# Turning query features one feed-forward unit later, with two query tiles instead of four in the last phase

## The chip, the cores and the metric

The kernel runs on one core of a Trainium2 chip. The time is device microseconds of the whole execution on that core, the median of several runs; a profile is one further execution, with its own time.

## What is computed

A linear attention with learned softmax features and a gated feed-forward layer, both on the same normalised input, for 2048 tokens of width 640, 32 heads of width 20, and a hidden width of 1536:

```python
xn = _layernorm(x, axis=-1)
# attention: q, k, v from xn @ wqkv; per head
pq = einsum("bhsd,hdf->bhsf", q, w_phi);  pk = einsum("bhsd,hdf->bhsf", k, w_phi)
phi_q = concat([softmax(pq), softmax(-pq)]);  phi_k = concat([softmax(pk), softmax(-pk)])
kv = einsum("bhsf,bhsd->bhfd", phi_k, v);  z = einsum("bhsf->bhf", phi_k)
o = einsum("bhqf,bhfd->bhqd", phi_q, kv) / (einsum("bhqf,bhf->bhq", phi_q, z)[..., None] + 1e-6)
s = o @ wo
# feed-forward
g = silu(gelu(xn @ w1 + b1) @ w2 + b2)
return x + s * g
```

## The kernel before

The program has three phases. Products of fp32 values are made from a high and a low part each (three matmuls, `PASSES`), so most operands are slabs with two halves.

**First phase**: normalisation, keys, values and queries of 16 tiles of 128 tokens. A query tile ends as exponentials in DRAM (`e_dram`). The sums over the keys (`kvp`) build up in one PSUM bank.

**Feed-forward phase**: 12 units, `unit` = 6 * h + g. Half h is one half of the tokens, group g two of the twelve blocks of the hidden width. A unit computes the hidden values in seven parts (`part`, L649, one Strassen-like scheme over two token groups and two blocks) and then the down projection (`down`, L678) for two token groups into `ys`. Between the matmuls, the loop's body calls generators, each up to its next `yield`, so that the other engines' work stands at fixed places in program order:

- `q_norm(t, ef)` turns the exponentials of query tile t into normalised features: `ez` on GpSimd (L724), sums on VectorE (L365), the reciprocal of the denominator, scaling on GpSimd (L370), a transpose on VectorE (L741), and four stores to `phi_t` on SyncE's queue (L745). `q_load` (L718) fetches the exponentials. `QN` says which tiles are turned in which unit.
- `w1_forms` makes the next unit's five W1 tiles on ScalarE (L429) and GpSimd (L418, L430). Units 2 to 4 also store theirs (`w1_store`, L445), and units 7 to 9 fetch them back for the unit that follows (`w1_back`, L451).
- `x_forms` makes, in units 0 to 3, sums of the input for the second half, stored by L711 and L712; `reload` fetches the second half's input in unit 5.

**Last phase**: four blocks of 512 tokens in the order `ORDER = (2, 3, 0, 1)`. `load_phi` (L764, L766) loads a block's features; `num` (L776, L783) multiplies them with the state of the keys into `oT` (VectorE's half is L780); `finish` (L829 to L836) makes one of five output tiles of a block: 16 matmuls with `wo`, the product with the gate (L831), the sum with the input (L832), the store (L836). For the blocks 2 and 3 the gates come from DRAM (`gt`), for 0 and 1 from `ys`. `load_res` asks for input and gate two tiles ahead. Between the tiles `late_q` turns the last query tiles, a step for every `next(lq)`. `load_wol` loads the last rows of `wo` and makes their low part.

From the feed-forward phase on, all engines run in the order in which the program is written (`manual_schedule`), with semaphores for the data. All loads and stores of this part are issued by SyncE, in program order: an instruction that waits for its data holds all behind it. Slabs (`slab`, 23 of them), rows (11) and PSUM banks (8) are pools: a new tile waits until an earlier one's last reader is done.

Of the kernel before, what the change touches and what calls it, by code (L numbers as in the profile page):

```python
# [15 lines left out]
P = 128  # L16
NT = S // P
NCH = 4
# [28 lines left out]
def hedgehog_gated_mlp_kernel(ctx: ExitStack, tc: tile.TileContext, x, xt_in, wqk, bd, wv, wo, w1, b1, w2, b2, out_t):  # L47
# [33 lines left out]
    def slab(dt, name, shape=(P, 2, D)):  # L81
        return slabs.tile(list(shape), dt, tag="S", name=name)

    def row(shape, dt, name):
        return rows.tile(shape, dt, tag="R", name=name)
# [4 lines left out]
    def bankB(name="pB"):  # L90
        return pools["B"].tile([P, 512], F32, tag="B", name=name)
# [271 lines left out]
    def head_sums(ef, tag):  # L363
        ss = small.tile([P, 64], F32, tag=tag, name=tag)
        nc.vector.tensor_reduce(ss[:], ef.rearrange("p (g d) -> p g d", d=DH), axis=AX.X, op=OP.add)  # L365
        return ss

    def scale_heads(ef, rc):
        e3 = ef.rearrange("p (g d) -> p g d", d=DH)
        nc.gpsimd.tensor_tensor(e3, e3, rc[:, :, None].to_broadcast([P, 64, DH]), op=OP.mult)  # L370
# [67 lines left out]
    def w1_dict(tiles):  # L438
        wa, wc, wd, wb = tiles
        return dict(A11=(wa, 0), A12=(wa, 256), A1k=(wa, 512), A22=(wb, 0), A2k=(wb, 256),  # L440
                    S1=(wc, 0), S2=(wc, 256), S3=(wd, 0), S4=(wd, 256), tiles=tiles)
# [5 lines left out]
    def w1_back(g):  # L447
        out = []
        for o, n in W1OFF:
            sl = slab(F32R, "w1s")  # L450
            nc.sync.dma_start(sl[:, :, :n].bitcast(F32), w1_dram[g][:, :, o:o + n])  # L451
            out.append(sl)
        return w1_dict(out)
# [139 lines left out]
    t = NT - 1  # L593
# [121 lines left out]
    def q_load(t):  # L715
        e = slab(F32, "eq")
        ef = e[:].rearrange("p a b -> p (a b)")
        nc.sync.dma_start(ef, e_dram[t])  # L718
        return ef

    def q_norm(t, ef):
        ez = slab(F32, "ez")
        zv = ez[:].rearrange("p a b -> p (a b)")
        nc.gpsimd.tensor_tensor(zv, ef, zf, op=OP.mult)  # L724
        yield
        rc = head_sums(ef, "rc")
        nc.vector.reciprocal(rc[:], rc[:])
        yield
        dn = head_sums(zv, "dn")
        yield  # L730
        nc.vector.tensor_tensor(dn[:], dn[:], rc[:], op=OP.mult)
        d3 = dn[:].rearrange("p (h s) -> p h s", s=2)
        den = small.tile([P, 32], F32, tag="den", name="den")
        nc.vector.scalar_tensor_tensor(den[:], d3[:, :, 0], DEN_EPS, d3[:, :, 1], op0=OP.add, op1=OP.add)
        nc.vector.reciprocal(den[:], den[:])
        r3 = rc[:].rearrange("p (h s) -> p h s", s=2)
        nc.vector.tensor_tensor(r3, r3, den[:, :, None].to_broadcast([P, 32, 2]), op=OP.mult)  # L737
        yield
        scale_heads(ef, rc)
        yield  # L740
        nc.vector.transpose(ef, ef)  # L741
        c, i = divmod(t, TPC)
        dst = phi_t[c].rearrange("(b j) (t a i) -> t a j b i", j=32, a=4, i=32)[i]
        for a in range(4):
            nc.sync.dma_start(dst[a], ef[32 * a:32 * a + 32, :].rearrange("p (b i) -> p b i", i=32))  # L745

    def load_wol():
        raw = row([P, D], F32, "raw")
        for r in range(3):
            nc.sync.dma_start(raw[40 * r:40 * r + 40, :], wo[640:680, :])  # L750
        wol_h = row([P, D], F32R, "wolh")
        wol = row([P, D], F32R, "wol")
        nc.vector.tensor_copy(wol_h[:120, :], raw[:120, :])
        nc.vector.scalar_tensor_tensor(wol[:120, :], wol_h[:120, :].bitcast(F32), midsel[:120, :], raw[:120, :],
                                       op0=OP.mult, op1=OP.add)
        return wol


    def load_phi(c, js):
        out = {}  # L760
        for j in js:
            ph = slab(F32, "phT", (P, 2, CW))
            if j < 5:
                nc.sync.dma_start(ph[:120], phi_t[c][240 * j:240 * j + 240, :].rearrange("(e p) t -> p e t", p=120))  # L764
            else:
                nc.sync.dma_start(ph[:80, 0], phi_t[c][1200:, :])  # L766
            out[j] = ph
        return out
# [20 lines left out]
    JA, JB = (0, 1, 2), (3, 4, 5)  # L789
# [2 lines left out]
        return ([home.tile([P, 2, 512], F32R, tag="S" if home is slabs else "L", name="oT") for _ in range(5)],  # L792
                slab(F32R, "oTl", (P, 2, 512)))

    xres, gates = {}, {}
    ORDER = (2, 3, 0, 1)

    def load_res(i):
# [18 lines left out]

    def finish(c, d, oT, last):
        steps = [(wo_s[j][:, b, d * P:(d + 1) * P], oT[0][j][:, a, :]) for j in range(5) for a, b in PASSES]
        steps.append((wol[:120, d * P:(d + 1) * P], oT[1][:120, 1, :]))  # L820
        xr, gt = xres.pop((c, d)), gates.pop((c, d))
        end = last and d == KC - 1
        parts = (slice(0, 384), slice(384, 512)) if end else (slice(0, W2), slice(W2, 512))
        for k, sl in enumerate(parts):
            if end or k == 0:
                mv = sl if end else slice(0, 512)
                ps = bankB()
                for n, (w, o) in enumerate(steps):
                    nc.tensor.matmul(ps[:, mv], w, o[:, mv], start=n == 0, stop=n == 15, skip_group_check=True)  # L829
            g = gt[:, sl]  # L830
            nc.vector.tensor_tensor(g, ps[:, sl], g, op=OP.mult)  # L831
            (nc.vector if last else nc.gpsimd).tensor_tensor(xr[:, sl], g, xr[:, sl], op=OP.add)  # L832
            if last:
                nc.sync.dma_start(out_t[d * P:(d + 1) * P, c * CW + sl.start:c * CW + sl.stop], xr[:, sl])
        if not last:
            nc.sync.dma_start(out_t[d * P:(d + 1) * P, c * CW:(c + 1) * CW], xr[:])  # L836


    zf, none = None, iter(())
    QN = {1: (8,), 2: (9,), 3: (10,), 4: (11,), 5: (12,), 7: (13, 14), 8: (15, 0), 9: (1, 2), 10: (3,)}  # L840
    units = NH * NG

    def w2_raw(g):
        return [load_raw(w2[f * P:(f + 1) * P, :]) for f in range(g * GF, (g + 1) * GF)]
# [6 lines left out]
    open_psum(ctx, B=8)  # L851
    ffn = ExitStack()
    ffn.enter_context(tc.manual_schedule())
    qe, xg, qlast = {}, none, none
    for unit in range(units):
        h, g = divmod(unit, NG)
        f1, f2 = g * GF, g * GF + 1
        more, back = unit + 1 < units, NG + 1 < unit + 1 < units - 1
        qs = [q_norm(t, qe.pop(t)) for t in QN.get(unit, ())]
        q1, q2 = (qs + [none, none])[:2]  # L860
        next(q1, None)
# [9 lines left out]
            wo_r = [load_raw(wo[j * P:(j + 1) * P, :]) for j in range(5)]  # L871
            phi = load_phi(ORDER[0], range(6))
        xo, xg = xg, (x_forms(unit, *x_back(unit)) if unit < SLOTS else none)
        for t in QN.get(unit + 1, ()):
            qe[t] = q_load(t)
        if 2 <= unit < NG - 1:
            w1_store(unit, w1g)
        if unit == NG + 1:
# [39 lines left out]
        h21 = act_lo(*h21)  # L918
        nc.vector.tensor_tensor(c12, u2[:], c12, op=OP.add)
        h12 = act(c12, f1)  # L920
        next(qlast, None)
        qlast = q2
        next(xo, None)
        silu(3)
        hs = ((h11, h21), (None, h22))
# [9 lines left out]
        w1f = w1_forms(w1r) if more and not back else none  # L935
        if back:
            w1g = w1_back((unit + 1) % NG)
        next(w1f, None)
        dn = down(g, w2g, hs, 0)
        next(dn)  # L940
# [23 lines left out]
        next(dn)  # L964
        next(dn)
        next(q2, None)
        next(q1, None)
        next(dn)
        next(q2, None)
        next(dn)  # L970
# [1 line left out]
        if unit == NG - 1:  # L972
            held = list(ys)
            ys[:] = [None] * KC
    wol = load_wol()
    oT = new_oT(late)
    phin = load_phi(ORDER[1], JA)
    qe[4] = q_load(4)
    load_res(0)
    load_res(1)  # L980

    def first_num():
        num(phi, oT, JA)
        yield
        yield
        num(phi, oT, JB)
        yield
# [5 lines left out]
    gate(1)  # L993

    def late_q():
        qn = q_norm(4, qe.pop(4))
        next(qn)
        for t in range(4, 8):
            if t < 7:
                qe[t + 1] = q_load(t + 1)  # L1000
            next(qn)
            yield
            next(qn)
            yield
            next(qn)
            next(qn)
            yield
            next(qn, None)
            if t < 7:
                qn = q_norm(t + 1, qe.pop(t + 1))  # L1010
                next(qn)
            yield

    lq = late_q()
    for ci, c in enumerate(ORDER):
        if ci + 1 < NCH:
            oTn = new_oT(late if ci % 2 else slabs)
        for d in range(KC):
            load_res(ci * KC + d + 2)
            finish(c, d, oT, ci == NCH - 1 and d >= 3)  # L1020
            next(lq, None)
            gate(ci * KC + d + 2)
            if ci == 0 and d % 2 == 0:
                next(lq, None)
            if ci + 1 < NCH and d in (1, 3):
                num(phin, oTn, JA if d == 1 else JB)
            if ci + 2 < NCH and d >= 3:
                phin.update(load_phi(ORDER[ci + 2], JA if d == 3 else JB))
            next(lq, None)
        if ci + 1 < NCH:  # L1030
            oT = oTn
    ffn.close()
# [50 lines left out]
```

## Time and profile before

| | |
|---|---|
| median of 3 runs | 694.87 us (690.53 to 695.24) |
| profiled execution, its own time | 692.98 us |
| its span, first to last instruction | 691.2 us |
| TensorE busy | 666.4 us (96%) |
| mean granted TensorE clock | 0.984 |
| DMA moved | 126.05 MB |

In the views, PE is TensorE (PEld its weight loads), DVE VectorE, ACT ScalarE, POOL GpSimd, SPq SyncE's queue of DMA issues. A line of a timeline has start, duration, engine, source line, operation, tiles, count, and in brackets the idle time before it and what ended it. A line of the chain of waits has start, duration and the piece of work. A line of waits says who waited for whom, for how long in total, how often, and the longest.

### The profile page before, as it was taken

How to read it: one execution, taken by the hardware profiler on the slowest of the kernel's cores; microseconds unless marked ns; L12 is line 12 of the kernel's file. 1: busy time of each engine (PE TensorE's matmuls, PEld its weight loads, DVE VectorE, ACT ScalarE, POOL GpSimd, SP SyncE). 2: the span in 40 equal slices, each digit the busy share in tenths (PEclk: the TensorE clock that was granted, in tenths of full speed). 3: DMA queues.
4: the chain of work that ended last, by engine and by line, in shares of the span. 5: the costliest groups of instructions: out<-in, count | busy, mean ns of one | idle time of the engine just before them, and what ended most of it. 6: DMA issues, size and time to landing. Idle time of an engine off the chain costs nothing.

```text
span 691.2 us, 11372 instructions
## 1 busy us (share of the span) xinstructions
PE 666.4 (96%) x4447; PEld 572.1 (83%) x4447; DVE 468.9 (68%) x720; ACT 227.2 (33%) x321; POOL 380.8 (55%) x351
## 2 busy tenths in 40 slices
PE   8999999999999999999898999999999999969798
PEld 8999999999999988887676888888888866636476
DVE  5787576878776567598566884578988646784222
ACT  3513213333233254424333247533134251103120
POOL 3653355767756486583858762726546542753231
PEclk9999999999999999999999999999999999989899
DMA  8820325451631536049587799465876699699943
GB/s 327 305 77 2 60 91 160 162 149 78 156 124 63 172 118 227 25 107 354 128 292 215 204 421 330 160 224 157 200 187 161 135 247 275 183 259 244 267 142 108
DMA packets 157950, 126.05 MB, mean 182 GB/s; under 512 B 88656, under 2 KB 125520, under 8 KB 157000
## 3 DMA queue, kind: packets, MB, share of 16 engines
q1 hardware_dynamic: 155592, 114.84, 57.8%
q10 hardware_dynamic: 2304, 10.49, 4.1%
q8 instruction: 35, 0.57, 0.3%
q14 instruction: 19, 0.16, 0.1%
HBM read 80.20 MB, written 45.10 MB: 181 GB/s over the span
## 4 chain that ended last, share of the span: by engine, by line
PE 69%; DMA 14%; DVE 6%; SPq 5%; POOL 3%; issue 2%; ACT 0%; DVEq 0%; POOLq 0%; ACTq 0%
PE pA L331 27%; PE pB L649 17%; PE pB L678 17%; DMA phT<-phi_t 6%; PE pB L829 5%; DMA w_dram<-w1s 2%; SPq L745 2%; DMA xt<-in_x_dram 2%; PE kv L402 2%; POOL w1s L430 1%; DVE eq L741 1%; POOL eq L370 1%; DMA folds<-in_wqk_dram 1%; DMA raw<-in_wv_dram 1%; DVE y L687 1%
## 5 line engine op out<-in xcount | busy, mean ns | idle before, releaser
L678 PE MATMUL pB<-hs,w2s 128*128 128x512 f32 x720 | 166.1, 390 | 1.2 <-DVE oT L780 1.2
L678 PEld LDWEIGHTS pB<-hs,w2s 128*128 128x128 f32 x720 | 135.3, 188 | 31.0 <-DVE oT L780 2.1
L649 PE MATMUL pB<-xp,w1s 128*128 128x512 f32 x324 | 85.2, 402 | 6.6 <-DVE pB L910 5.2
L649 PEld LDWEIGHTS pB<-xp,w1s 128*128 128x128 f32 x324 | 62.4, 194 | 21.3 <-DVE pB L910 6.0
L649 PE MATMUL pB<-xd,w1s 128*128 128x512 f32 x324 | 79.3, 389 | 0.0
L829 PE MATMUL pB<-oT,wo 128*128 128x512 f32 (+2 forms) x315 | 76.1, 394 | 2.7 <-DVE oT L780 2.7
L829 PEld LDWEIGHTS pB<-oT,wo 128*128 128x128 f32 x315 | 59.3, 194 | 20.5 <-DVE oT L780 4.0
L649 PEld LDWEIGHTS pB<-xd,w1s 128*128 128x128 f32 x324 | 60.8, 188 | 12.7
L357 ACT ACTIVATE e<-e 128x1280 f32<-128x1280 f32 x32 | 40.7, 1272 | 91.2 <-POOL e L352 90.7
L687 DVE TENSOR_TENSOR y<-pB,y 128x512 f32<-128x512 f32 x100 | 63.4, 677 | 5.4 <-PE pB L678 5.4
L370 POOL TENSOR_TENSOR eq<-eq,rc 128x1280 f32<-128x1280 f32 x16 | 37.9, 2371 | 50.0 <-DVE rc L737 40.7
L370 POOL TENSOR_TENSOR e<-e,rc 128x1280 f32<-128x1280 f32 x16 | 39.0, 2438 | 47.6 <-DVE rc L390 47.4
L352 POOL TENSOR_TENSOR e<-nr,e 128x640 f32<-128x640 f32 x32 | 44.2, 1383 | 30.8 <-DVE nr L351 25.9
L331 PE MATMUL pA<-wv,xp 128*128 128x320 f32 x384 | 60.5, 310 | 0.3 <-POOL wv L147 0.3
L331 PE MATMUL pA<-wk,xp 128*128 128x320 f32 x384 | 59.7, 310 | 0.0
L654 ACT ACTIVATE pB<-pB,b1t 128x512 f32<-128x512 f32 x48 | 31.8, 662 | 83.4 <-DVE pB L910 33.6
L331 PE MATMUL pA<-wq,xp 128*128 128x320 f32 x384 | 58.8, 309 | 0.2 <-DVE nr L351 0.2
L331 PEld LDWEIGHTS pA<-wv,xp 128*128 128x128 f32 x384 | 57.0, 188 | 0.5 <-POOL wv L147 0.5
L331 PEld LDWEIGHTS pA<-wq,xp 128*128 128x128 f32 x384 | 56.9, 188 | 0.4 <-PE pA L331 0.4
L331 PEld LDWEIGHTS pA<-wk,xp 128*128 128x128 f32 x384 | 56.9, 188 | 0.1
L724 POOL TENSOR_TENSOR ez<-eq,zrep 128x1280 f32<-128x1280 f32 x16 | 47.2, 2950 | 1.2 <-issue 1.2
L430 POOL TENSOR_TENSOR w1s<-raw,w1s 128x640 fp32r<-128x640 f32 (+1 forms) x18 | 25.7, 1429 | 28.0 <-ACT w1s L429 23.8
(138 smaller groups left out, 997.1 us busy)
## 6 DMA issues: line engine op xcount, KB each, us to landing
raw<-in_w_dram SPq DMA_DIRECT2D x42, 320.0 KB, 4.1
e_dram<-e ACTq DMA_DIRECT2D x16, 640.0 KB, 3.4
eq<-e_dram SPq DMA_DIRECT2D x16, 640.0 KB, 6.2
phi_t<-eq SPq DMA_DIRECT2D x64, 160.0 KB, 3.7
phT<-phi_t SPq DMA_DIRECT2D x20, 480.0 KB, 11.4
xt<-in_x_dram SPq DMA_DIRECT2D x16, 320.0 KB, 5.2
xres<-in_xt_dram SPq DMA_DIRECT2D x20, 256.0 KB, 6.0
out_dram<-xres SPq DMA_DIRECT2D x18, 256.0 KB, 5.8
```

Of the source, the lines that this page charges most:

```text
L331: nc.tensor.matmul(ps[:, hf, :HALF], stat_x(q, o, k, a), ws[k][:, b, hf * HALF:(hf + 1) * HALF], start=n == 0, stop=n == 3 * KC - 1)
L352: nc.gpsimd.tensor_tensor(e5[:, :, :, 1, :], nr[:, :, :, None].to_broadcast([P, 2, 16, DH]), e5[:, :, :, 0, :], op=OP.subtract)
L357: nc.scalar.activation(ef, ef, AF.Exp)
L370: nc.gpsimd.tensor_tensor(e3, e3, rc[:, :, None].to_broadcast([P, 64, DH]), op=OP.mult)
L402: nc.tensor.matmul(ps[32 * e:32 * e + 32, 40 * s:40 * s + 40], v[:, 21 * h:21 * h + 32], phi[:, 40 * h:40 * h + 40], start=t == 0 and s == ...
L430: nc.gpsimd.tensor_tensor(sl[:, 1, :n], src, sl[:, 0, :n].bitcast(F32), op=OP.subtract)
L649: nc.tensor.matmul(bank[ch][:], tl[:, a, off + wo_:off + wo_ + P], mov(blk, b), start=new and n == 0, stop=n == len(mms) - 1, skip_group_c ...
L654: nc.scalar.activation(ps, ps, AF.Gelu_apprx_tanh, bias=b1t[:, f:f + 1])
L678: nc.tensor.matmul(ps[:], ws[i][:, b, d * P:(d + 1) * P], hs[o][i][:, a, :], start=i == n == 0, stop=(i, n) == (GF - 1, 2), skip_group_che ...
L687: nc.vector.tensor_tensor(y, ps[:], y, op=OP.add)
L724: nc.gpsimd.tensor_tensor(zv, ef, zf, op=OP.mult)
L829: nc.tensor.matmul(ps[:, mv], w, o[:, mv], start=n == 0, stop=n == 15, skip_group_check=True)
```

## The change

The last steps of `q_norm` are split: the transpose and the four stores are now separate steps, and both are taken in the unit after the one that did the rest (`turn(qdone)` twice, in the middle of the unit: the transposes after the last activation, the stores after the W1 forms of the next unit have been asked for). The loads of the next unit's queries move from the start of a unit to the place behind these stores. Tiles 4 and 5, which were turned in the last phase, are turned in units 10 and 11, so that `late_q` finishes tile 5 and turns 6 and 7. The steps of `late_q` are called at other places, the features of the third and fourth block are loaded at a block's tiles 1 and 3, and the raw rows of `wol` are loaded in unit 11 and made into `wol` between the first two groups of query products.

```diff
@@ q_norm
         nc.vector.transpose(ef, ef)
+        yield
         c, i = divmod(t, TPC)
...
-    def load_wol():
+    def wol_raw():
         raw = row([P, D], F32, "raw")
         for r in range(3):
             nc.sync.dma_start(raw[40 * r:40 * r + 40, :], wo[640:680, :])
+        return raw
+
+    def make_wol(raw):
...
-    QN = {1: (8,), 2: (9,), 3: (10,), 4: (11,), 5: (12,), 7: (13, 14), 8: (15, 0), 9: (1, 2), 10: (3,)}
+    QN = {1: (8,), 2: (9,), 3: (10,), 4: (11,), 5: (12,), 7: (13, 14), 8: (15, 0), 9: (1, 2), 10: (3, 4), 11: (5,)}
+
+    def turn(qs):
+        for q in qs:
+            next(q, None)
@@ the loop over the units
         xo, xg = xg, (x_forms(unit, *x_back(unit)) if unit < SLOTS else none)
-        for t in QN.get(unit + 1, ()):
-            qe[t] = q_load(t)
         if 2 <= unit < NG - 1:
             w1_store(unit, w1g)
...
         h12 = act(c12, f1)
-        next(qlast, None)
-        qlast = q2
+        turn(qdone)
         next(xo, None)
...
         if back:
             w1g = w1_back((unit + 1) % NG)
+        if not more:
+            wolr = wol_raw()
+        turn(qdone)
+        qdone = qs
+        for t in QN.get(unit + 1, ()):
+            qe[t] = q_load(t)
         next(w1f, None)
         dn = down(g, w2g, hs, 0)
...
         next(q2, None)
-        next(q1, None)
         next(dn)
@@ after the loop
-    wol = load_wol()
     oT = new_oT(late)
     phin = load_phi(ORDER[1], JA)
-    qe[4] = q_load(4)
+    qe[6] = q_load(6)
...
     def first_num():
         num(phi, oT, JA)
         yield
+        wols.append(make_wol(wolr))
         yield
...
     def late_q():
-        qn = q_norm(4, qe.pop(4))
+        turn(qdone)
+        turn(qdone)
+        qn = q_norm(6, qe.pop(6))
         next(qn)
-        for t in range(4, 8):
-            if t < 7:
-                qe[t + 1] = q_load(t + 1)
+        qe[7] = q_load(7)
+        yield
+        for t in (6, 7):
...
+            next(qn)
+            yield
             next(qn, None)
...
@@ the loop over the blocks
             next(lq, None)
             gate(ci * KC + d + 2)
-            if ci == 0 and d % 2 == 0:
+            if ci == 0 and d < 4 or ci == 1 and d == 0:
                 next(lq, None)
             if ci + 1 < NCH and d in (1, 3):
                 num(phin, oTn, JA if d == 1 else JB)
-            if ci + 2 < NCH and d >= 3:
-                phin.update(load_phi(ORDER[ci + 2], JA if d == 3 else JB))
-            next(lq, None)
+            if ci + 2 < NCH and d in (1, 3):
+                phin.update(load_phi(ORDER[ci + 2], JA if d == 1 else JB))
```

More of the change, by code (lines that the diff above doesn't have):

```diff
@@ L793, in new_oT @@
                 slab(F32R, "oTl", (P, 2, 512)))
-    xres, gates = {}, {}
+    xres, gates, wols = {}, {}, []
     ORDER = (2, 3, 0, 1)
@@ L819, in finish @@
         steps = [(wo_s[j][:, b, d * P:(d + 1) * P], oT[0][j][:, a, :]) for j in range(5) for a, b in PASSES]
-        steps.append((wol[:120, d * P:(d + 1) * P], oT[1][:120, 1, :]))
+        steps.append((wols[0][:120, d * P:(d + 1) * P], oT[1][:120, 1, :]))
         xr, gt = xres.pop((c, d)), gates.pop((c, d))
@@ L853, in hedgehog_gated_mlp_kernel @@
     ffn.enter_context(tc.manual_schedule())
-    qe, xg, qlast = {}, none, none
+    qe, xg, qdone = {}, none, []
     for unit in range(units):
@@ L1007, in late_q @@
             yield
+            next(qn)
+            yield
             next(qn, None)
-            if t < 7:
-                qn = q_norm(t + 1, qe.pop(t + 1))
+            if t == 6:
+                qn = q_norm(7, qe.pop(7))
                 next(qn)
```

## The prediction

> **What bounds the kernel now.** I read the page's first parts, then the busy time cut at the starts of the feed-forward units (each unit begins with the first L649 matmul of its seven parts), then TensorE's timeline for its gaps, then the chain of waits behind each gap, then SyncE's queue and the DMA share.
>
> ```profile
> span 691.2 us, 11372 instructions
> PE 666.4 (96%) x4447; PEld 572.1 (83%) x4447; DVE 468.9 (68%) x720; ACT 227.2 (33%) x321; POOL 380.8 (55%) x351
> ...
> 326.80:358.62 31.82, 28.04 (x116) 22.38 (x115) 21.46 (x32) 10.96 (x18) 21.57 (x19) 0.95 0.78 232
> 358.62:389.47 30.85, 28.03 (x116) 22.41 (x114) 20.49 (x30) 11.76 (x19) 27.38 (x23) 0.94 0.67 200
> 519.04:544.88 25.84, 25.84 (x116) 21.40 (x115) 23.00 (x34) 8.98 (x15) 20.45 (x15) 1.00 0.52 121
> 544.88:570.70 25.82, 25.82 (x115) 18.16 (x113) 10.97 (x18) 11.57 (x19) 8.93 (x6) 1.00 1.00 237
> ```
>
> The columns of a stretch are its length, then busy time of PE, PEld, DVE, ACT, POOL, the granted clock, the DMA share and GB/s. TensorE is the bound: a unit that never waits (519.04, unit 10) is 25.84 us of matmuls end to end. Only what keeps TensorE idle or at a lower clock can be won. Units 3 and 4 take 31.82 and 30.85 us: 3.78 and 2.82 us idle, and the same 116 matmuls took 28.04 instead of 25.84.
>
> ```profile
> 341.24 3.88 PE L649 MATMUL pB<-xp,w1s 128*128 128x512 f32 x9 [2.60 <-DVE pB L910]
> 372.11 3.91 PE L649 MATMUL pB<-xp,w1s 128*128 128x512 f32 x9 [2.57 <-DVE pB L910]
> ...
> 572.30 5.74 PE L678 MATMUL pB<-hs,w2s 128*128 128x512 f32 x24 [1.19 <-DVE oT L780]
> 585.25 2.79 PE L776 MATMUL pB<-phT,bdk 120*64 120x512 f32 x12
> 607.39 1.69 PE L829 MATMUL pB<-oT,wo 128*128 128x512 f32 x4 [2.74 <-DVE oT L780]
> 617.79 4.67 PE L776 MATMUL pB<-phT,bdk 120*64 120x512 f32 x12 [3.71 <-DMA phT<-phi_t]
> 647.80 1.08 PE L776 MATMUL pB<-phT,bdk 120*64 120x512 f32 x4 [3.47 <-DMA phT<-phi_t]
> 668.47 3.58 PE L829 MATMUL pB<-oT,wo 128*128 128x512 f32 x15
> 672.13 3.58 PE L829 MATMUL pB<-oT,wo 128*128 128x512 f32 x15
> 683.09 2.79 PE L829 MATMUL pB<-oT,wo 128*128 128x384 f32 x15
> 687.52 0.28 PE L829 MATMUL pB<-oTl,wol 120*128 120x128 f32 x1
> ```
>
> The other gaps lie in the last phase. It starts at 578.04 (572.30 + 5.74) and ends at 687.80: 109.8 us. Its work without waits: 19 output tiles of 3.66 us (668.47 to 672.13), a split last one of 4.71 (683.09 to 687.80), six groups of query products of 2.79 (585.25): 69.5 + 4.7 + 16.7 = 90.9. So 18.9 us are lost there, part of it clock: the 12 matmuls after the 3.71 us gap took 4.67 instead of 2.79.
>
> Why unit 3 is late, from the chain of waits:
>
> ```profile
> 313.38 1.98 SPq L718
> ...
> 317.51 8.72 DMA w_dram<-w1s
> ...
> 328.51 3.52 POOL w1s L430 x3
> 332.03 2.33 POOL eq L370
> ...
> 334.39 1.51 DVE eq L741
> ```
>
> SyncE was held at the query load L718 until 315.36, so the store of unit 2's W1 forms (L445) went out late and landed 8.72 us after 317.51; GpSimd needed those slabs for the next forms (L430); the query's scaling (L370) came after them; and VectorE sat in front of the query's transpose (L741) while TensorE needed u2, u3 and c22 behind it. The SyncE queue shows what put the loads so late:
>
> ```profile
> 305.30 2.46 SPq L745 DMA_DIRECT2D phi_t<-eq  x4
> 307.81 2.30 SPq L153 DMA_DIRECT2D raw<-in_w_dram  x4
> ...
> 534.29 13.21 SPq L745 DMA_DIRECT2D phi_t<-eq  x8
> ...
> SPq L745 <- DVE eq L741: 119.5, 13, 14.0
> ```
>
> The feature stores L745 stand ahead of the next unit's weight loads and wait for the transpose: 119.5 us in 13 waits. Unit 2 starts at 300.96 (326.80 - 25.84), but its loads only go out at 307.81; before unit 11 the queue is held to 547.50.
>
> **Part 1, transposes and stores one unit later.** No instruction is added; three pieces move. (a) On SyncE the loads of a unit no longer queue behind L745 of the unit before: unit 2's can issue before 301 instead of 307.81, and the W1 store follows them directly, since the query load is behind it too. That is over 10 us earlier than 315.36, more than the 3.78 us that unit 3 idled, and its waits hang on this one POOL sequence. (b) VectorE no longer meets the transpose between the scaling and u2, so L370 being late blocks nobody there. So units 3 and 4 should return to 25.84: 5.98 + 5.01 = **11.0 us** gained; the bounds are 0 (slabs still short) and 11.0.
>
> A rule of the Trainium skill weighs on this size: TensorE: Matmul & The Clock Gate, Part 1: The HAM clock gate, has the clock halved after at least one idle window of about 3.4 us. The gaps here are 2.60 and 2.57 us and still the nine matmuls behind took 3.9 us, so the trace differs; by the page only the idle 6.6 us would come back and the result would be 4.4 us higher.
>
> (c) In units with two queries both transposes now stand between c12 and the low half of h12 on VectorE:
>
> ```profile
> 531.27 13.76 PE L678 MATMUL pB<-hs,w2s 128*128 128x512 f32 x60
> ...
> 532.16 0.69 DVE L919 TENSOR_TENSOR pB<-u,pB 128x512 f32<-128x512 f32 x1
> ...
> 534.80 0.68 DVE L660 TENSOR_TENSOR hs<-pB,hs 128x512 fp32r<-128x512 f32 x1
> ```
>
> L660 moves by 1.5 us and ends at 537.0; TensorE comes to h12 after the first 30 of the 60 matmuls, at 538.1. Cost 0 with 1.1 us of cover to spare; with that gone, up to 1.5 us in each of units 8, 9 and 10.
>
> **Part 2, tiles 4 and 5 in units 10 and 11.** Unit 10 gets a second query.
>
> ```profile
> L724 POOL TENSOR_TENSOR ez<-eq,zrep 128x1280 f32<-128x1280 f32 x16 | 47.2, 2950 | 1.2 <-issue 1.2
> ...
> 525.96 3.09 POOL L147 TENSOR_TENSOR w2s<-raw,w2s 128x640 fp32r<-128x640 f32 x2
> ...
> 538.93 1.02 POOL L430 TENSOR_TENSOR w1s<-raw,w1s 128x384 fp32r<-128x384 f32 x1
> ```
>
> GpSimd: 2.95 (L724) ahead of the W1 forms and 2.33 (L370) behind: 20.45 becomes 25.7 of 25.84. The last form ends at 542.9 instead of 539.95, TensorE wants it at 544.88: hidden by 2 us; unit 11 (8.93 busy) takes up the tail. VectorE's tail shifts into unit 11 too, which has 10.97 of 25.82 busy and gets two transposes (1.5 each) and one query's sums. Cost 0, with a bound of 2 us. The slab pool (23) is the tight place: in unit 10, five y, zrep, two w2s, four hs, four stored or waiting eq, two ez, st, four w1s and the next eq make 24, so one form waits for an ez or eq to come free; I take that as inside the 2 us.
>
> **Part 3, wol.** Its raw rows are loaded in unit 11 and made between the product groups.
>
> ```profile
> 570.16 0.51 DVE wolh L753
> ...
> 635.63 3.80 DMA phi_t<-eq
> ...
> 642.19 7.53 DMA phT<-phi_t
> ```
>
> At 570.16 the cast came late for its DMA, L780 waited behind it, and TensorE 1.19 us. The queue in front of that DMA starts some 3 to 6 us earlier now: **1.2 us** gained.
>
> **Part 4, the last phase.** Four queries become two; phi of the third block is loaded at the first block's tiles 1 and 3 instead of 3 and 4, the fourth's a block later likewise. Before, the fourth block's loads came behind a late store (635.63, then 642.19, then the 3.47 us gap). Half the VectorE work between the L780 goes, so the 2.74 us gap should close. Against this stands the DMA:
>
> ```profile
> 471.00:475.00 4.00, 4.00 (x19) 3.34 (x18) 3.60 (x5) 1.26 (x2) 4.00 (x3) 1.00 1.16 177
> 475.30:480.00 4.70, 4.70 (x22) 3.92 (x21) 2.77 (x5) 2.52 (x4) 4.70 (x3) 1.00 1.01 376
> 545.00:657.00 112.00, 99.57 (x402) 66.32 (x401) 60.29 (x101) 26.40 (x42) 46.74 (x38) 0.94 0.97 244
> 590.00:604.00 14.00, 14.00 (x62) 9.82 (x61) 9.56 (x14) 1.79 (x3) 11.17 (x8) 1.00 0.71 172
> ```
>
> A tile's store alone (0.66 MB) takes 4 us at 177 GB/s. From 545 to 657, when the last phi load is in, DMA moved 112 x 244 = 27.3 MB at a share of 0.97. The change takes only two query loads out of it (1.3 MB), as tile 3's and 4's stores now fall in the middle of unit 11 and 5's into the first block. 26.0 MB at 251 GB/s is 103.6 us: from 541.5, where the queue is no longer held, to 645. TensorE without waits would want the last load at 576.85 + 2 x 23.88 (a block: 5 x 3.66 + 2 x 2.79) + 4 x 3.66 + 2.79 = 642.0. So DMA and TensorE run about level and some wait stays. I leave 6 us: one gap like the 3.71 and 3.47 measured, 4 us, and 1.9 of slow clock behind it (4.67 against 2.79). Gain 18.9 - 6 = **12.9 us**; bounds 0 and 18.9.
>
> **Sum.** The profiled execution took 692.98 us, 1.78 over its span; it lies 1.9 under the median of 694.87 and inside 690.53 to 695.24, so its differences carry over. 692.98 - 11.0 - 1.2 - 12.9 = 667.9; I say **668**.
>
> **Rivals.** (A) The last phase runs clean: another 6 us, 662. For it: between 590 and 604 the DMA share was only 0.71, which can be filled. Against it: the level sum above.
>
> (B) DMA decides the last phase.
>
> ```profile
> DVE gt L831 <- DMA gt<-g_dram: 13.2, 4, 6.0
> ```
>
> The gates (gt) and xres are asked for only two tiles ahead and now queue behind phi loads that come earlier; VectorE waits in L831 for gt (13.2 us already), L780 behind it is late, and TensorE stops at the start of the second and third block. Two gaps of 5 us with 1.7 us of clock each leave 13.4 of the 18.9: 692.98 - 12.2 - 5.5 = 675.
>
> (C) The feed-forward part isn't mended: eq stays in its slab until a store that now goes out in the middle of the next unit has landed, GpSimd's forms wait for that slab instead of the W1 store's, and units 3 and 4 stay late: 692.98 - 1.2 - 12.9 = 679.
>
> (D) Slower: the query load now stands behind the stores, and GpSimd takes ez (2.95) and the first w2 split (1.55) before the unit's down projection, 12.23 us after the start (531.27 - 519.04). If eq lands X us after the unit's start, TensorE waits X - 7.7 in each of ten units with queries. My X goes by the DMA: from about 14 us into the unit (L919 ends at 532.85) it brings the W1 forms back (2.1 MB at 376 GB/s, 5.6 us), then two tiles' stores (8) and a load (0.66 MB, 1.7), 29.3 us after a start that comes round again at 25.84: about +4 in units 9 and 10, before the start elsewhere. It eats the gain from X of about 10 in all ten units; 11 there would give 668 + 33 = 701. The Trainium skill's page DMA: Bandwidth & Descriptors, Queues, rings and completion order, has each DMA engine take descriptors in ring order, which speaks for (D): no load overtakes those stores; no row here shows one that does.
>
> (E) The order moves and the time doesn't, other stalls taking the places: 686 to 700.
>
> **Chances.** Forecast 0.40 (664 to 672), A 0.15, B 0.22, C 0.08, E 0.07, D 0.08. Faster by over 1% (7 us, about what a measurement here can tell from no change): 0.85; within 1%: 0.07; slower: 0.08. The range goes from A less the spread of the runs (2.5 us) to past B and C with a gap more: 659 to 685.
>
> **What would show it.** Right: units 3 and 4 at 25.84 us with clock 1.00; L745 waits far under 119.5 us; no gap at the wol cast; phT loads of the third block issued before 595; one small gap left, at oT L780 or phT. Wrong: gaps before L649 at POOL w1s or DVE L910 in units 3, 4 or 11 (C); POOL L724 waiting for eq in units 9 and 10 (D); DVE L831 waiting for gt over 13 us and gaps at block starts (B).

## The result, and the profile after

The changed kernel takes 668.79 us (median of 4 runs, 667.85 to 668.94) against 694.32 for the kernel before (690.53 to 695.24): a ratio of 0.964, interval 0.960 to 0.968. The profiled execution took 667.85 us, with a mean granted clock of 0.999.

First the page's head, then the busy time by stretch, with the columns of the prediction's table (length, then busy time of PE, PEld, DVE, ACT, POOL, the clock, the DMA share and GB/s). The stretches are units 2, 3, 4, 10 and 11, the stretch in which the DMA has most to do, and the last phase.

```profile
span 666.1 us, 11389 instructions
PE 657.0 (99%) x4447; PEld 568.3 (85%) x4447; DVE 472.1 (71%) x720; ACT 228.1 (34%) x321; POOL 379.9 (57%) x351
...
300.86:326.70 25.84, 25.84 (x116) 21.40 (x114) 22.11 (x30) 10.33 (x16) 20.10 (x17) 1.00 0.76 211
326.70:352.54 25.84, 25.84 (x116) 21.40 (x114) 22.11 (x30) 10.23 (x17) 20.09 (x17) 1.00 0.94 283
352.54:378.38 25.84, 25.84 (x116) 21.40 (x114) 22.12 (x32) 10.64 (x17) 20.33 (x18) 1.00 0.77 231
507.95:533.79 25.84, 25.84 (x116) 21.40 (x115) 22.89 (x34) 9.83 (x16) 21.49 (x14) 1.00 0.62 161
533.79:559.66 25.87, 25.87 (x115) 18.15 (x113) 24.48 (x36) 11.61 (x19) 18.16 (x10) 1.00 0.96 233
534.00:646.00 112.00, 107.98 (x462) 73.48 (x461) 66.87 (x111) 30.52 (x49) 50.14 (x44) 1.00 0.96 249
565.69:662.70 97.01, 92.99 (x408) 65.17 (x407) 41.60 (x79) 18.16 (x29) 36.08 (x40) 1.00 0.87 232
```

Units 3 and 4 (31.82 and 30.85 us before) are now 25.84 us, without a gap and at full clock. The last phase takes 97.0 us instead of 109.8, and all that TensorE still idles behind unit 1 lies there. (The same line of the program has another number in each kernel: L780, L831 and L745 of the kernel before are L784, L835 and L746 here, and one off in some of the experiments.) In its timeline (start, duration, and in brackets the idle time and what ended it):

```profile
609.52 1.08 PE L780 MATMUL pB<-phT,bdk 120*64 120x512 f32 x4 [0.69 <-DMA phT<-phi_t]
611.75 1.07 PE L787 MATMUL pB<-phT,bdl 80*64 80x512 f32 x4 [1.15 <-issue]
621.26 1.20 PE L833 MATMUL pB<-oT,wo 128*128 128x512 f32 x4 [2.07 <-DVE oT L784]
```

That is 3.9 us of gaps, where the three of the last phase before took 9.9 (2.74, 3.71, 3.47). No slow clock follows: the four matmuls behind the longest take 1.20 us, the fifteen of the next tile 3.59. SyncE's queue shows the new order in unit 2 (first lines), ahead of the last phase and ahead of the third block:

```profile
293.16 2.63 SPq L153 DMA_DIRECT2D raw<-in_w_dram  x4
...
298.40 6.37 SPq L445 DMA_DIRECT2D w_dram<-w1s  x4
316.05 2.46 SPq L746 DMA_DIRECT2D phi_t<-eq  x4
318.62 0.81 SPq L718 DMA_DIRECT2D eq<-e_dram  x1
...
531.05 2.46 SPq L153 DMA_DIRECT2D raw<-in_wo_dram  x5
...
582.83 2.38 SPq L768 DMA_DIRECT2D phT<-phi_t  x3
```

Unit 2's weight loads go out at 293.16 (307.81 before), ahead of its feature stores, now L746; the rows of wo at 531.05 instead of behind 547.50; the third block's features from 582.83 on. The waits say the same of the whole program, and show the new price, VectorE waiting for the gates in L835:

```profile
SPq L746 <- DVE eq L741: 68.1, 9, 14.4
DVE gt L835 <- DMA gt<-g_dram: 29.5, 6, 7.0
```

The queue's waits for the transpose fell from 119.5 us to 68.1; VectorE's for gt rose from 13.2 us to 29.5.

### The profile page after: what moved, and what is told of

It reads as the page before. It is cut to its first block, busy times and chain, and to the rows that moved or that the text cites. A ratio compares the mean times of both kernels' runs of the same rounds, so it can differ in the third digit from the quotient of the medians.

```text
span 666.1 us, 11389 instructions
## 1 busy us (share of the span) xinstructions
PE 657.0 (99%) x4447; PEld 568.3 (85%) x4447; DVE 472.1 (71%) x720; ACT 228.1 (34%) x321; POOL 379.9 (57%) x351
## 4 chain that ended last, share of the span: by engine, by line
PE 88%; DMA 7%; DVE 2%; SPq 1%; POOL 1%; issue 0%; ACT 0%; DVEq 0%; POOLq 0%
PE pA L331 28%; PE pB L678 25%; PE pB L649 22%; PE pB L833 8%; PE pB L780 2%; PE kv L402 2%; DMA xt<-in_x_dram 2%; DMA phT<-phi_t 1%; DMA raw<-in_wv_dram 1%; DMA folds<-in_wqk_dram 1%; DMA xres<-in_xt_dram 1%; SPq L746 1%; DMA gt<-g_dram 1%; PE pA L172 1%; POOL wv L147 0%
## 5 line engine op out<-in xcount | busy, mean ns | idle before, releaser
L678 PEld LDWEIGHTS pB<-hs,w2s 128*128 128x128 f32 x720 | 134.9, 188 | 29.5 <-DVE oT L784 0.8
L649 PE MATMUL pB<-xp,w1s 128*128 128x512 f32 x324 | 81.3, 389 | 0.0
L833 PE MATMUL pB<-oT,wo 128*128 128x512 f32 (+2 forms) x315 | 73.8, 385 | 2.1 <-DVE oT L784 2.1
L833 PEld LDWEIGHTS pB<-oT,wo 128*128 128x128 f32 x315 | 57.4, 188 | 18.7 <-DVE oT L784 4.4
L649 PEld LDWEIGHTS pB<-xp,w1s 128*128 128x128 f32 x324 | 60.8, 188 | 12.6
L370 POOL TENSOR_TENSOR eq<-eq,rc 128x1280 f32<-128x1280 f32 x16 | 37.9, 2369 | 53.8 <-DVE rc L737 36.6
L370 POOL TENSOR_TENSOR e<-e,rc 128x1280 f32<-128x1280 f32 x16 | 39.0, 2438 | 47.6 <-DVE rc L390 47.4
```

Source lines behind the costliest of these rows:

```text
L649: nc.tensor.matmul(bank[ch][:], tl[:, a, off + wo_:off + wo_ + P], mov(blk, b), start=new and n == 0, stop=n == len(mms) - 1, skip_group_c ...
L678: nc.tensor.matmul(ps[:], ws[i][:, b, d * P:(d + 1) * P], hs[o][i][:, a, :], start=i == n == 0, stop=(i, n) == (GF - 1, 2), skip_group_che ...
```

## The experiments

**Theory 1**: a feature store that waits for its transpose on SyncE's queue holds the weight and feature loads behind it. That costs time at two places, units 3 and 4 and the stretch from unit 10 on. What is left in the last phase is DMA work that ends too late. Rivals: the place of the query loads is what matters in the units; the last phase gains by the smaller VectorE work between the L784 rather than by its transfers; a query that lands late costs by way of GpSimd (D of the prediction).

The experiments were timed in three batches, with the kernel before in each: its medians were 692.9, 692.42 and 692.08 us, against 694.32 beside the changed kernel. A difference of about 2 us between kernels of different batches therefore says nothing. Stretches of time are read from one profiled execution of each kernel.

**The two parts, one at a time.** `e1_units_only` keeps the new order in the units, but the old tile plan and last phase; `e2_tiles_only` has the new tile plan and last phase with the old order in the units.

```diff
# e1, against the changed kernel (late_q, load_phi's places and wol as before, too)
-    QN = {..., 10: (3, 4), 11: (5,)}
+    QN = {..., 10: (3,)}
# e2, against the changed kernel
         nc.vector.transpose(ef, ef)
-        yield
...
+        for t in QN.get(unit + 1, ()):
+            qe[t] = q_load(t)
         if 2 <= unit < NG - 1:
...
-        turn(qdone)
-        qdone = qs
-        for t in QN.get(unit + 1, ()):
-            qe[t] = q_load(t)
...
+        next(q1, None)
         next(dn)
```

> Only the order inside the units is the new one (transposes and stores one unit later, query loads behind them); tiles 4 to 7 stay in the last phase, with its old steps, old loads and old wol. Additive theory (the prediction's terms): units 3 and 4 at 25.84 us, 11.0 us less than before, 682 on the profile's scale, all waits of the last phase still there (18.9 us). Rival: the last phase was late because the queue was held before it; then it shrinks too and the time is under 677.

> Only the other half: tiles 4 and 5 in units 10 and 11, the new last phase and the new wol, while transposes and stores stand at the end of their own unit and query loads at a unit's start, as before. Additive theory: 692.98 - 1.2 - 12.9 = 679, units 3 and 4 still 31 to 32 us. Rival: stores ahead of wo and phi loads in unit 11 cost the last phase its gain: 685 or more.

Measured: e1 680.8 us (679.33 to 681.45), e2 684.06 (683.17 to 684.81), before 692.9 with them. TensorE's timeline of e1 has these gaps in the last phase, and the stretches of units 3 and 4 in e2 are still long:

```profile
605.87 4.01 PE L780 MATMUL pB<-phT,bdk 120*64 120x512 f32 x8 [4.71 <-DMA phT<-phi_t]
636.88 1.98 PE L780 MATMUL pB<-phT,bdk 120*64 120x512 f32 x4 [3.39 <-DMA phT<-phi_t]
```

```profile
313.92:344.86 30.94, 28.07 (x115) 22.39 (x114) 20.81 (x30) 10.17 (x17) 20.39 (x17) 0.94 0.77 228
344.86:375.15 30.29, 26.45 (x115) 21.24 (x114) 20.67 (x29) 10.29 (x17) 20.65 (x18) 1.00 0.80 243
```

e1 gains 12.1 us by its median. That is the prediction's 11.0 + 1.2: the gap at wol is gone in e1 too, though its wol lines are the old ones, so it was the new order in the units that closed it, not the earlier load. From the first output tile on e1 takes 109.8 us, as the kernel before does (109.9): the rival, by which the last phase shrinks with the units alone, falls.

By the spans (691.2 before, 666.1 after) e1 gains 11.7 and e2 9.8, together 21.5 of the 25.1 that both give at once. And of e2's 9.8 the units give 1.4 (61.23 us for units 3 and 4 against 62.67), which leaves 8.4 for the new plan and last phase; on top of the mended units they are worth 25.1 - 11.0 = 14.1. So about 5.7 us of the second part seem to hang on the first: as a sum, e2 would have come to 692.9 - 14.1 = 679. By the traces 3.8 of the 5.7 lie between the start of unit 11 and the first output tile (35.5 us in e2, 31.7 in the changed kernel), 1.2 behind it (98.3 against 97.2), and 0.8 ahead of unit 0, where the kernels are the same. The cuts below show on which piece of the first part this hangs.

**Which move in the units does it.** `e3_query_loads_first` only puts the query loads back at the unit's start; `e4_stores_first` only puts transposes and stores back, and leaves the query loads in the middle.

```diff
# e3, against the changed kernel
+        for t in QN.get(unit + 1, ()):
+            qe[t] = q_load(t)
         if 2 <= unit < NG - 1:
...
-        for t in QN.get(unit + 1, ()):
-            qe[t] = q_load(t)
         next(w1f, None)
# e4, against the changed kernel
         nc.vector.transpose(ef, ef)
-        yield
...
         turn(qdone)
+        qdone = qs[1:]
...
-        turn(qdone)
-        qdone = qs
...
+        next(q1, None)
         next(dn)
```

> The changed kernel with the query loads back at the start of a unit, ahead of the W1 store; transposes and stores stay late. Theory 1 (the stores waiting for transposes in front of the loads made the W1 store late): within 2 us of the changed kernel, 667 to 671, units 3 and 4 at 25.84. Theory 2 (the query load's own wait for a slab, the L718 in the chain, made it late): units 3 and 4 late again by 2 to 6 us each, 673 to 680.

> The changed kernel with transposes and stores back at the end of their own unit (the second query's in the next unit), query loads staying in the middle. Theory 1: the loads queue behind the stores again, units 3 and 4 late by 5 to 6 us each: 678 to 682. Theory 2: within 3 us of the changed kernel, 667 to 672.

Measured: e3 667.66 us (666.27 to 668.97), no different from the changed kernel; e4 680.95 (679.04 to 682.08). In SyncE's queue of e4 the loads of unit 2 are back at their old time, with the W1 store behind them:

```profile
307.71 2.42 SPq L153 DMA_DIRECT2D raw<-in_w_dram  x4
...
311.52 7.67 SPq L445 DMA_DIRECT2D w_dram<-w1s  x4
```

In the kernel before the issues of the W1 store run from 315.41 to 318.77, here from 311.52 to 319.19: the store now has the place in the queue that the query load had, and its own issue takes long. So it is the move of the transposes and stores that does it. With them late the place of the query loads is worth nothing that can be measured; with them early it is worth 3.1 us (e2 against e4).

e4's time lies in the range that Theory 1 gave, but not as it was argued: units 3 and 4 are 2.2 and 3.9 us late instead of 5 to 6 each, and the rest lies from unit 11 on. And e4 moves a transpose and its store together, so it doesn't tell the two links apart that the prediction named: (a) the loads behind the store on SyncE, (b) the transpose in front of u2 on VectorE. No run moves one without the other.

**Where the stores cost.** `e11_stores_first_to_unit_9` puts transposes and stores back for the tiles of units 1 to 9 only, `e12_stores_first_from_unit_10` for those of units 10 and 11 only (tiles 3, 4, 5).

```diff
# e11, against the changed kernel; e12: "if t not in (3, 4, 5)" and "if unit == 10"
         nc.vector.transpose(ef, ef)
-        yield
+        if 3 <= t < 8:
+            yield
...
+        if unit < 10:
+            next(q1, None)
         next(dn)
```

> Tiles of units 1 to 9 are transposed and stored where the kernel before does it, those of units 10 and 11 where the changed kernel does it. Theory 1 (a store that waits for its transpose holds the loads behind it, and this costs time at two places, units 3 and 4 and the last phase, each with its own stores): units 3 and 4 lose the 6.0 us that e4_stores_first loses there, the last phase stays as in the changed kernel (97 us from the first output tile to the end): 668.8 + 6 = 674 to 676 us. Rival (the last phase loses because DMA work was pushed back all through the units, not because of the stores ahead of unit 11): the last phase loses 4 to 5 us here too, 679 to 681 us.

> The opposite cut: tiles 3, 4 and 5 (units 10 and 11) are transposed and stored where the kernel before does it, all others where the changed kernel does it. Theory 1: units 3 and 4 stay at 25.84 us, SyncE is held ahead of unit 11 to about 546 us and again to about 565, the loads of wo and of the first block's features go out some 14 us later than in the changed kernel, and the last phase ends 4 to 6 us later: 673 to 675 us. Rival (pushed back all through the units): as the changed kernel, 668 to 669 us.

Measured: e11 676.06 us (672.54 to 677.57), e12 675.64 (674.98 to 677.12), with ratios of 0.977 and 0.978 to before. Against the changed kernel that is 7.3 and 6.9 us (Theory 1 gave 6 and 4 to 6), together 14.1, where e4, which has both, loses 12.2. In e11 (first fence: the stretch of unit 3, then TensorE's timeline) units 3 and 4 are 2.15 and 4.97 us over 25.84 (27.99, and 354.95 to 385.76, where unit 5 begins), and the last phase from the first output tile on is 96.6 us against 97.2 in the changed kernel. In e12 (second fence: SyncE, VectorE, TensorE) units 3 and 4 are 25.84 each. From the start of unit 11 to the first output tile it takes 36.9 us against 31.7, from there to the end 99.6 against 97.2:

```profile
326.96:354.95 27.99, 26.49 (x116) 21.24 (x114) 21.86 (x30) 10.23 (x16) 19.15 (x17) 1.00 0.87 253
385.76 1.52 PE L649 MATMUL pB<-xp,w1s 128*128 128x512 f32 x6
572.91 3.56 PE L834 MATMUL pB<-oT,wo 128*128 128x512 f32 x15
...
669.23 0.28 PE L834 MATMUL pB<-oTl,wol 120*128 120x128 f32 x1
```

```profile
539.35 2.42 SPq L747 DMA_DIRECT2D phi_t<-eq  x4
541.80 2.74 SPq L153 DMA_DIRECT2D raw<-in_wo_dram  x5
...
549.91 12.20 SPq L747 DMA_DIRECT2D phi_t<-eq  x4
562.21 1.65 SPq L752 DMA_DIRECT2D raw<-in_wo_dram  x3
...
548.38 1.50 DVE L741 STREAM_TRANSPOSE eq<-eq 128x1280 f32<-128x1280 f32 x1
568.37 0.49 DVE L758 CAST wolh<-raw 120x640 fp32r<-120x640 f32 x1 [8.63 <-DMA phT<-phi_t]
...
544.64 2.35 PE L649 MATMUL pB<-xp,w1s 128*128 128x512 f32 x9 [0.74 <-DVE pB L917]
556.99 1.08 PE L781 MATMUL pB<-phT,bdk 120*64 120x512 f32 x4 [1.05 <-DMA phT<-phi_t]
570.43 5.32 PE L834 MATMUL pB<-oT,wo 128*128 128x512 f32 x15 [1.84 <-DVE oT L785]
```

The store of tile 3 (539.35) waits for its transpose, and the rows of wo go out behind it at 541.80 instead of 531.05. The four stores of tile 4 then hold the queue for 12.20 us. That is not a wait for the transpose, which ends at 549.88: the issues themselves take so long, two of them 5.84 and 4.55 us, while the DMA share is between 1.01 and 1.08 (540 to 562). The rows of wol (L752) go out behind them, and VectorE waits 8.63 us in front of the oT that TensorE needs (the bracket names the phT loads issued right behind those rows). 1.84 us of gap follow, and 1.76 of slow clock in the first output tile. This is the old wol gap on a queue that is held longer: unit 10 has a second tile in the new plan, tile 4, and its stores stand ahead of the wol rows. In e2 they hold the queue for 12.87 us at the same place. So it costs time at two places, each with its own stores, as Theory 1 says, and 4.9 of the 5.7 us that e2 lacks lie at the second (from unit 11 on). But at the second place the wait for the transpose is only the start of it: stores and loads then meet where the DMA is busy all the time. The rival that the last phase suffers from DMA work pushed back all through the units falls with e11's unchanged last phase.

**Is it the transfers in the last phase?** `e5_half_gates` loads half of each gate and multiplies both halves by it (the right half of the gate values of blocks 2 and 3 is left out). `e9_late_stores_twice` writes the features of tiles 5, 6 and 7 twice. `e6_one_late_tile` starts the second half's tiles a unit earlier, so that only tile 7 is turned in the last phase; its first load stands at the start of unit 5. `e6b_load_behind_reload` is the same with that load in the middle of unit 5, behind `reload`.

```diff
# e5
-            nc.sync.dma_start(gates[c, d][:], g_dram[d, :, c - 2, :])
+            nc.sync.dma_start(gates[c, d][:, :W2], g_dram[d, :, c - 2, :W2])
# e9
-        for a in range(4):
+        for a in (0, 1, 2, 3) * (1 + (t in (5, 6, 7))):
# e6 and e6b
-    QN = {..., 7: (13, 14), 8: (15, 0), 9: (1, 2), 10: (3, 4), 11: (5,)}
+    QN = {..., 6: (13,), 7: (14, 15), 8: (0, 1), 9: (2, 3), 10: (4, 5), 11: (6,)}
...
-    qe[6] = q_load(6)
+    qe[7] = q_load(7)
# and late_q turns tile 7 alone; in e6, q_load(13) ahead of w1_store's place in unit 5
```

> Of each gate that comes from DRAM only the left half is loaded and used for both halves (the right half's values are left out): 1.3 MB less DMA in the first two blocks, about 5 us at 251 GB/s. Theory (what is left of the last phase's loss, 97.0 against 90.9 us, is DMA work that lands late): 2 to 5 us less, 664 to 667, VectorE's wait for gt (29.5 us) at most half. Rival (SyncE's order or VectorE's work sets it): 668 to 669.

> The stores of tiles 5, 6 and 7 are each issued twice, with the same data: 12 us more DMA work in the first two blocks. Theory (DMA and TensorE run level there): 8 to 12 us more, 677 to 681. Rival (the DMA has slack that the waits for its order hide): 0 to 3 us more.

> Query tiles one place earlier: tile 13 in unit 6 (which had none; loaded at the start of unit 5), then two in each of units 7 to 10, tile 6 in unit 11, and tile 7 alone in the last phase. One store (4 us of DMA) and one query load (1.7 us) fewer fall into the last phase. Theory (DMA): 3 to 5 us less, 664 to 666. Rival (no slab free, a unit late): 668 or more.

> As the one before, but tile 13's exponentials are asked for behind the reload of the second half's input (10 MB) in the middle of unit 5, so that they land X us after unit 6 has begun. By the prediction's rival D TensorE waits X - 7.7 in unit 6; with about 14 us of backlog X is 5 to 12, the wait 0 to 4 us. If the rival's path is wrong (another engine's wait comes first, VectorE's sum before u2 in this order), TensorE waits from X of about 6 on.

Measured: e5 665.21 us (664.95 to 665.72), e9 681.16 (679.51 to 682.78, just over what the theory gave), e6 662.91 (662.16 to 665.1), e6b 666.61 (665.71 to 667.51), before 692.42 with them. From the first output tile to the end the profiled executions take 97.2 us in the changed kernel, 94.6 in e5 (10 half gates, 1.3 MB less), 91.7 in e6 (one load and one store, 1.3 MB less), and 110.2 in e9 (three stores, 2.0 MB more). Three stores at 4 us each are 12; the stretch grew by 13.0. TensorE's timeline of e9:

```profile
598.89 2.08 PE L833 MATMUL pB<-oT,wo 128*128 128x512 f32 x4 [5.68 <-DVE oT L784]
601.19 5.07 PE L833 MATMUL pB<-oT,wo 128*128 128x512 f32 x15
...
633.03 2.08 PE L833 MATMUL pB<-oT,wo 128*128 128x512 f32 x4 [5.24 <-DVE oT L784]
635.33 5.07 PE L833 MATMUL pB<-oT,wo 128*128 128x512 f32 x15
```

These are the gaps of 5 us at the starts of the second and third block, with slow clock behind them, of which rival B spoke, once there is that much more to move. VectorE's waits for gt, in e9, e5 and e6:

```profile
DVE gt L835 <- DMA gt<-g_dram: 47.0, 7, 10.7
```

```profile
DVE gt L835 <- DMA gt<-g_dram: 27.5, 6, 7.0
```

```profile
DVE gt L835 <- DMA gt<-g_dram: 34.2, 7, 7.5
```

They are no measure of the loss: in e5, where they were expected to fall to half, they went from 29.5 to 27.5 us only, and e6 waits longer than the changed kernel, though its TensorE never stops in the last phase:

```profile
566.18:657.69 91.51, 91.51 (x408) 65.71 (x407) 35.16 (x71) 18.16 (x29) 30.83 (x38) 1.00 0.82 229
```

What counts is whether an L784 that TensorE needs stands right behind such a wait. Work on VectorE cannot explain e9 and e5, which leave its instructions as they are. e6 takes away one tile's VectorE work too, so its 5.5 us are not shown to be DMA's alone, and how much of the changed kernel's own gain here came from VectorE's smaller work was not measured apart.

e6, at 662.91 us (ratio to before 0.958, interval 0.952 to 0.963), beats the kernel before, and its slowest run (665.1) lies below the fastest of the changed kernel (667.85), which was timed in another batch. It is the changed kernel's plan one step further.

**A query that lands late.** In e6b the exponentials of tile 13 land 7.3 us after unit 6 starts at 404.48. VectorE, GpSimd and TensorE there:

```profile
411.77 1.49 DVE L365 TENSOR_REDUCE rc<-eq 128x64 f32<-128x1280 f32 x1 [6.40 <-DMA eq<-e_dram]
411.88 2.96 POOL L724 TENSOR_TENSOR ez<-eq,zrep 128x1280 f32<-128x1280 f32 x1 [9.19 <-DMA eq<-e_dram]
416.04 2.33 PE L649 MATMUL pB<-xp,w1s 128*128 128x512 f32 x9 [1.20 <-DVE pB L916]
```

TensorE waits 1.20 us, and not for the w2 split behind ez on GpSimd: VectorE's sum of the query (L365) stands ahead of u2, u3 and c22 (L916), and it is that row which comes late. By D's formula, X - 7.7 with X = 7.3, there would have been no wait. The way by VectorE starts to cost at X of about 6.1 (7.3 - 1.2). The rest of e6b's distance to e6 is a gap of 1.51 us in the last phase behind a gate, with 1.6 of slow clock.

## Why the prediction was right, step by step

**Units 3 and 4.** Forecast 11.0 us, and 5.98 + 5.01 came back: both units are 25.84 us long. That the late transposes and stores do it is shown (e4, e11); which of the two links, (a) or (b), is argued only. Two lines of TensorE's waits in the kernel before, all of them in units 3 and 4, say what each can explain:

```profile
PE pB L649 <- DVE pB L910: 5.2, 2, 2.6
PE pB L649 <- POOL w1s L430: 1.4, 2, 1.2
```

The 1.4 us are waits for the W1 forms themselves, so only (a) can have taken them away. The 5.2 us came from the late forms by way of the scaling and the transpose on VectorE, and as the chain stands either move could have kept them away. The page of the Trainium skill TensorE: Matmul & The Clock Gate, Part 1: The HAM clock gate, would have left 4.4 us of this in place; they came back with the gaps, as the trace of before said. One reason given was superfluous: that the query load now stands behind the W1 store. e3 puts it back and loses nothing.

**Transposes ahead of h12 on VectorE.** Forecast cost 0, cover 1.1 us. In VectorE's timeline of unit 8

```profile
469.98 2.90 DVE L741 STREAM_TRANSPOSE eq<-eq 128x1280 f32<-128x1280 f32 x2
...
473.38 0.67 DVE L660 TENSOR_TENSOR hs<-pB,hs 128x512 fp32r<-128x512 f32 x1
```

both transposes stand ahead of L660, which ends at 474.05. The down projection begins at 468.51, and 30 matmuls of it last 6.8 (half of 13.6): h12 is wanted at about 475.3. No gap, 1.3 us of cover.

**Unit 10.** Forecast cost 0 with 2 us of cover; GpSimd 25.7 us busy. It was 21.49 in that stretch: the prediction counted all of the second query's work into unit 10, but its scaling (L370) runs at 538.22 and the next w2 split at 543.47, in unit 11. The last W1 form ended at 529.11 + 1.03 = 530.14, and unit 11 began at 533.79: 3.65 us of cover.

```profile
529.11 1.03 POOL L430 TENSOR_TENSOR w1s<-raw,w1s 128x384 fp32r<-128x384 f32 x1
```

**wol.** 1.2 us, gone as forecast; e1 closes it without the new wol lines, and in e12 it is back, longer, with the queue held.

**The last phase.** Forecast 12.9 of 18.9 us; 109.8 became 97.0, so 12.8. The step "DMA and TensorE run about level" is borne out: the forecast had 26.0 MB in 103.6 us, and in the 103.6 us from 530.5 on, 11.0 earlier as the units are, the DMA moves 25.8 MB at 249 GB/s with a share of 0.99. The 6 us left are 4.0 of idle time (97.01 - 92.99) and 2.1 of longer busy time (92.99 - 90.9); 4 and 1.9 were left for them. That the two sizes fit is luck, for they are made otherwise. The idle time is three small gaps instead of one like those before: the gap of 2.74 us at the start of the second block closed, as was argued, but one of 2.07 opened at the start of the third, where rival B had one. And the 1.9 us of slow clock did not come; the granted clock of the stretch is 1.00. Of the 2.1 some 0.6 stand in e6 as well, where the stretch is 91.51 us without any wait, since the tile behind each group of products starts slower (3.70 us instead of 3.58, six times): 90.9 was the wrong floor by that much. Another 0.5 is one slower tile at 589.62, and the rest lies in the matmuls around the three gaps.

**The sum was right, its split less so.** The terms were added as if each part gave its own. The base of the last one, 26.0 MB "from 541.5, where the queue is no longer held", held only with part 1 in place: without it the stores of tile 4, which the plan itself adds to unit 10, hold the queue for 12.20 us (e12) and 12.87 us (e2), and part 2 alone is worth 8.4 us instead of 14.1. For the whole change that cost nothing; a forecast for one half would have been wrong by it.

**The rivals.** A's 662 for a clean last phase is what e6 reaches (662.91) with one tile less in it. B's mechanism is present, gates late and L784 behind them, at 2 us instead of 10 here; e9 shows it at full size. C did not occur: units 3 and 4 have no gap at all. D's place was right and its way wrong. In unit 9, where X of 10 was the point of worry, GpSimd takes ez right behind the scaling, with no wait for eq:

```profile
485.10 2.37 POOL L370 TENSOR_TENSOR eq<-eq,rc 128x1280 f32<-128x1280 f32 x1 [4.94 <-PE pB L649]
487.43 2.95 POOL L724 TENSOR_TENSOR ez<-eq,zrep 128x1280 f32<-128x1280 f32 x1
```

## What to carry to other kernels

On a queue that runs in program order, a store that waits for its data is priced by the loads behind it, and not only by its own bytes: look in the queue's timeline for a long hold in front of loads, and try the store behind them first. Tell a wait for data from an issue that takes long while the DMA is busy; both held the queue here. Two parts of a change that share a queue need not add; undo each alone before giving each its share. When the DMA is level with the bound engine, count the bytes that fall in the last stretch: moving one tile's load and store out of it took away the last waits here.

## What the runs showed of the hardware that was not expected

TensorE's clock after a gap does not go by the gap's length alone. In the kernel before, gaps of 2.60 and 2.57 us were followed by nine matmuls in 3.88 and 3.91 us; in e11 one of 2.52 by nine in 3.66, in e2 one of 2.59 by nine in 2.35, in e4 one of 2.47 in 2.34 (undisturbed: 2.20). In e12 a gap of 1.84 us cost 1.76 more; in the changed kernel the four matmuls behind one of 2.07 took 0.1 more and the next fifteen 3.59; in e3 the four behind one of 2.19 took 0.1 more too, but the next fifteen 5.15.

```profile
368.65 3.66 PE L649 MATMUL pB<-xp,w1s 128*128 128x512 f32 x9 [2.52 <-DVE pB L917]
```

```profile
368.64 2.34 PE L649 MATMUL pB<-xp,w1s 128*128 128x512 f32 x9 [2.47 <-DVE pB L915]
```

The first line is of e11, the second of e4: the same matmuls of the same unit at the same time, with nearly the same gap. The page of the Trainium skill TensorE: Matmul & The Clock Gate, Part 1: The HAM clock gate, gives at least one idle window of about 3.4 us as the condition, and a window that runs free of the kernel. Gaps of half that length that cost clock do not agree with the first; that nearly equal gaps end so differently could come from the second, but no run here varied a gap's phase, and what decides it stays open. For a forecast on this kernel it means that the clock behind a gap of 1.5 to 2.8 us was worth between 0 and 1.8 us in these traces, and that the 4.4 us of clock in the 11.0 were not bound to be there.
